# Attention on one core: two key tiles per stretch of values, a score bank copied out by VectorE, keys split later

## The chip, the cores and the metric

The kernel runs on one core of a Trainium2 chip. The metric is the device time of one execution in microseconds (us). TensorE (PE, its weight loads PEld), VectorE (DVE), ScalarE (ACT), GpSimd (POOL) and SyncE (SP, which issues most DMAs) each take their own instructions in order and wait for one another by semaphores. Matmul results land in PSUM, eight banks of 128x512 fp32.

## The reference

```python
def _A_ref(x, wq, wk, wv, wo):            # x 1x2048x448, 16 heads of 28, one shared key and value head
    q = (x @ wq).reshape(B, S, H, Dh).transpose(0, 2, 1, 3)
    k = x @ wk
    v = x @ wv
    scores = jnp.einsum("bhqd,bkd->bhqk", q, k) * (Dh ** -0.5)
    p = softmax(scores)
    o = jnp.einsum("bhqk,bkd->bhqd", p, v)
    return o.transpose(0, 2, 1, 3).reshape(B, S, H * Dh) @ wo

def _B_ref(x, w1, w2, w3, w4):
    h = gelu(layernorm(x) @ w1)
    hs = token_shift(h) @ w2              # four channel groups, moved by +1, -1, +2, -2 tokens
    x1 = x + hs
    return x1 + gelu(layernorm(x1) @ w3) @ w4

g = sigmoid((x * gate_w).sum(-1, keepdims=True))
return g * _A_ref(x, ...) + (1 - g) * _B_ref(x, ...)
```

All is fp32.

## The kernel before

The order of every engine's instructions is the order in which the code writes them; nothing is rearranged. Most matmuls are made of three faster ones (fp32r): an operand is split into a high part `h` and a low part `l`, and high x high, high x low and low x high are added up.

**Start, 0 to about 130 us.** Queries, keys, values and the mixer's first half. Queries with keys and values in their spare rows go to DRAM (`qd`). `stage_w2` for the third token block calls `third(t)` between its tiles. There `load_k(b)` (eight DMAs, L332) reads a quarter of the keys from `qd` into one buffer `kf`, and `split_k(b)` on GpSimd (L336, L337) writes `kH` and `kL` from it. `stage_w2` for the last block calls `weights(t)`: it splits the first chunks of the MLP's weights (`split_w3`, in which GpSimd clears a part of `w3h`, L106) and issues the loads of the next (`load_w34`, L550).

**MLP, about 130 to 420 us.** Four blocks `b` of 512 tokens; in each, 14 tiles `f`: `w3_part` (11 matmuls, L130 to L134, two gelus), and for tile `f - 2` `w4_part` (12 matmuls). In tiles 10 and 11, DVE normalises the next block through the buffer `xn`. In block 1, `khd` (a few keys of each head) is put together, the first query tile is loaded and split; from block 2 on, `fill` does the parts of the first unit's maximum.

**Attention, from about 420 us.** 16 units `u`, each four heads by 512 queries, 16 key tiles `kt` of 128 keys. For each key tile there are 12 score matmuls (three splits, four heads side by side in row tiles of the array), into four of seven banks in rotation (`bank` takes the first of the list and puts it at its end). ScalarE takes the exponential of each bank (L832) into a tile `p`. `pv_group` multiplies `p` of the key tile two before with the values, in fp32, four heads side by side in column tiles, adding up over all 16 key tiles in an eighth bank. Beside that, in key tiles set by lists:

- `max_part` (four a unit) and `max_end` make a bound on the next unit's scores from 64 keys, which goes into spare rows of `qh` by DMA.
- After a unit, `sums_begin` copies the result to `o` and sends the sums by DMA; `recip` in key tile 3 and `norm` in key tile 6 divide by them. The reciprocals make a round trip through DRAM (`rd`, `rb`). GpSimd then splits the result.
- `wo_job` (three fp32r matmuls, four times a unit) is the output projection; DVE adds it up in `ot` (L778). In unit 0 four leftovers of the MLP, `w4_job`, stand in its place.

The end divides the last unit by another way, tests whether any sum was too large, and holds a branch that computes attention again with a full maximum.

Of the kernel before, what the change touches and what calls it, by code (L numbers as in the profile page):

```python
# [9 lines left out]
F32 = mybir.dt.float32  # L10
# [6 lines left out]
P = 128  # L17
# [15 lines left out]
MK = 64  # L33
# [3 lines left out]
def f32(ap):  # L37
    return ap.bitcast(F32)
# [3 lines left out]
def gated_mix_kernel(  # L42
# [41 lines left out]
    def mm_tile(name):  # L84
        return psA.tile([P, 512], F32, tag="mm", bufs=2, name=name)
# [114 lines left out]
    def max_part(u, t, tile_of):  # L200
        if t == 0:
            mx_of[u] = late.tile([P, 4, 4], F32, tag="mr", bufs=1, name=f"mr_{u}")
        ps = tile_of(f"m_{u}_{t}")[:, 0:4 * MK].rearrange("p (j k) -> p j k", j=4)
        nc.tensor.matmul(ps, qh_of[u][:, t * P:(t + 1) * P], khd, start=True, stop=True)  # L204
        nc.vector.reduce_max(mx_of[u][:, :, t], ps, axis=AX.X)  # L205
# [32 lines left out]
    with tc.tile_pool(name="s1b", bufs=1) as s1b, \  # L238
# [77 lines left out]
        kf = s1b.tile([P, 512], F32, name="kf")  # L316
        nc.gpsimd.memset(kf, 1.0)

# [9 lines left out]
        def load_k(b):  # L328
            for r in range(4):
                for g, n in ((0, 16), (1, DH - 16)):  # L330
                    at = 32 * r + 16 * g
                    nc.sync.dma_start(kf[at:at + n, :], rest(g, n, b))  # L332

        def split_k(b):
            cols = slice(512 * b, 512 * b + 512)
            nc.gpsimd.tensor_copy(kH[:, cols], kf)  # L336
            nc.gpsimd.tensor_tensor(kL[:, cols], kf, f32(kH)[:, cols], ALU.subtract)  # L337
# [191 lines left out]
        load_k(0)  # L529
# [77 lines left out]
    with tc.tile_pool(name="s2", bufs=1, reuse_waits="tile") as s2, \  # L607
# [5 lines left out]
        fills = [lambda t=t: max_part(0, t, max_tile if t % 2 else misc_tile) for t in range(4)]  # L613
        fills += [lambda: max_end(0)]
# [30 lines left out]
        for b in range(NB):  # L645
            acc = [ps2.tile([P, 512], F32, tag="acc", bufs=4, name=f"acc_{b}_{t}") for t in range(4)]
            gs = {}
            for f in range(NF):
# [24 lines left out]
                if b == 1 and f == 1:  # L673
# [4 lines left out]
                if b == 1 and f == 5:  # L678
                    q_split(0, qh0, ql0)
                if f >= 2:  # L680
                    for t in range(4):
                        w4_part(f - 2, t, gs[f - 2], acc)
                        if b > 1 and t % 2 == 0 and f < NF - 1:
                            fill()
# [15 lines left out]
    with tc.tile_pool(name="s3", bufs=1, reuse_waits="tile") as s3, \  # L700
            tc.tile_pool(name="ps3", bufs=1, space=PSUM, reuse_waits="tile") as ps3:
        woh = s3.tile([P, 4, D], F32R, name="woh")
        wol = s3.tile([P, 4, D], F32R, name="wol")

        banks = [mm_tile("bank_0"), mm_tile("bank_1"), misc_tile("bank_2")]
        banks += [ps3.tile([P, 512], F32, name=f"bank_{i}") for i in range(3, 7)]

# [26 lines left out]
        def sums_begin(u, pv):  # L734
            o = s3.tile([P, 512], F32, tag="o", bufs=2, name=f"o_{u}")
            nc.vector.tensor_copy(o, pv)
# [15 lines left out]
        def norm(u, o, rb):  # L752
            on = s3.tile([P, 512], F32, tag="onf", bufs=2, name=f"on_{u}")
            nc.vector.tensor_mul(on, o, rb)  # L754
            onh = s3.tile([P, 512], F32R, tag="onh", bufs=2, name=f"onh_{u}")
            onl = s3.tile([P, 512], F32R, tag="onl", bufs=2, name=f"onl_{u}")
            nc.gpsimd.tensor_copy(onh, on)  # L757
            nc.gpsimd.tensor_tensor(onl, on, f32(onh), ALU.subtract)
            on_of[u] = (onh, onl)
# [3 lines left out]
        def wo_job(u, t, end=None):  # L763
            b, g = divmod(u, NG)
            n = 4 * b + t
            tok = slice(t * P, (t + 1) * P)
            onh, onl = on_of[u]
            ps = bank(f"job_{n}")[:, 0:D]
            nc.tensor.matmul(ps, onh[:, tok], woh[:, g, :], start=True, stop=False)  # L769
            nc.tensor.matmul(ps, onh[:, tok], wol[:, g, :], start=False, stop=False)  # L770
            nc.tensor.matmul(ps, onl[:, tok], woh[:, g, :], start=False, stop=True)  # L771
# [3 lines left out]
            if end:  # L775
                end(t, n, ps, before)
                return
            nc.vector.scalar_tensor_tensor(ot_of[n], ps, gg[:, n:n + 1], before, op0=ALU.mult, op1=ALU.add)  # L778
            if g == NG - 1:
                nc.sync.dma_start(out[0, n * P:(n + 1) * P, :], ot_of[n])  # L780

        woraw = s3.tile([P, 4, D], F32, name="woraw")
        nc.sync.dma_start(woraw, wo.rearrange("(g p) n -> p g n", p=P))
        nc.gpsimd.tensor_copy(woh, woraw)
        nc.gpsimd.tensor_tensor(wol, woraw, f32(woh), ALU.subtract)
# [13 lines left out]
        p_of, pv_of, sums, norms = {}, {}, [], []  # L799

        def pv_group(k):
            u, kt = divmod(k, NT)
            if kt == 0:
                pv_of[u] = max_tile(f"pv_{u}")
            pv = pv_of[u]
            ps = p_of.pop(k)
            for j in range(4):
                nc.tensor.matmul(pv[32 * j:32 * j + 32, :], vext[:, kt, :], ps[j],  # L808
                                 start=(kt == 0), stop=(kt == NT - 1), tile_position=(0, 32 * j))
            if kt == NT - 1 and u < NU - 1:  # L810
                sums.append(sums_begin(u, pv_of.pop(u)))

        WO_AT = (8, 10, 12, 14)
        M_AT = (1, 3, 4, 5)
        M_FIRST = (5, 7, 9, 10)
        LAG = 2

        for k in range(NU * NT + LAG):
            u, kt = divmod(k, NT)
            if k < NU * NT:  # L820
                if kt == 13 and u + 2 < NU:
                    q_begin(u + 2)
                    q_fetch(u + 3)
                bs = [bank(f"s_{4 * k + j}") for j in range(4)]
                for i in range(3):
                    for j in range(4):
                        for _, _, w, a in score(u, bs[j], j, slice(kt * P, (kt + 1) * P), i=i):
                            nc.tensor.matmul(bs[j], w, a, start=(i == 0), stop=(i == 2), tile_position=(32 * j, 0))  # L828
                p_of[k] = []
                for j in range(4):  # L830
                    p = s3.tile([P, 512], F32, tag="p", bufs=PB, name=f"p_{4 * k + j}")
                    nc.scalar.activation(p, bs[j], AF.Exp, scale=SCALE)  # L832
                    p_of[k].append(p)
                if kt == 3 and sums:
                    norms.append(recip(*sums.pop()))
                if kt == 6 and norms:
                    norm(*norms.pop())
                if kt in WO_AT:
                    t = WO_AT.index(kt)
                    if u:  # L840
                        wo_job(u - 1, t)
                    else:
                        w4_job(t)
                m_at = M_AT if u else M_FIRST
                if u + 1 < NU and kt in m_at:
                    t = m_at.index(kt)
                    max_part(u + 1, t, bank)
                    if t == 3:
                        max_end(u + 1)
            if k >= LAG:  # L850
                pv_group(k - LAG)
# [3 lines left out]
        pv = pv_of.pop(u)  # L855
        o = s3.tile([P, 512], F32, tag="o", bufs=2, name=f"o_{u}")
        onh = s3.tile([P, 512], F32R, tag="onh", bufs=2, name=f"onh_{u}")
        onl = s3.tile([P, 512], F32R, tag="onl", bufs=2, name=f"onl_{u}")
        on_of[u] = (onh, onl)
# [18 lines left out]
        def tail_back(t):  # L878
            nc.tensor.transpose(tq[t], on4[:, t], ident)
            nc.scalar.copy(onh[:, toks[t]], tq[t])  # L880

        def tail_low(t):
            nc.vector.tensor_sub(onl[:, toks[t]], tq[t], f32(onh)[:, toks[t]])
# [20 lines left out]
        for t in range(4):  # L904
            nc.scalar.copy(o[:, toks[t]], pv[:, toks[t]])
# [14 lines left out]
        tail_low(0)  # L920
        tail_on(3)
        tail_low(1)
# [6 lines left out]
        tail_low(2)  # L929
        tail_wo(0)  # L930
        tail_back(3)
        tail_low(3)
        tail_wo(1)
        tw = max_tile("worst_t")[0:1, 0:P]
# [10 lines left out]
        with tc.If(again > 0, label="redo"):  # L945
            for b in range(NB):
                for g in range(NG):
# [5 lines left out]
                    pv = max_tile(f"pv2_{u}")  # L953
# [9 lines left out]
                    norm(*recip(*sums_begin(u, pv), False))  # L963
                    for t in range(4):
                        wo_job(u, t)
# [51 lines left out]
```

## Time and profile before

| | |
|---|---|
| median of 3 runs | 994.31 us (994.22 to 994.57) |
| profiled execution | 995.8 us |
| its span, first to last instruction | 994.0 us |
| mean granted TensorE clock over the span | 0.989 |
| TensorE, ScalarE, VectorE, GpSimd busy | 970.8, 651.9, 287.1, 107.5 us |

Names in the lines shown: a row of the timeline gives start, duration, engine, line, operation, tiles written <- tiles read, shapes and count; in brackets the idle time before it and what ended it. A window's row gives its length, the busy time of PE, PEld, DVE, ACT and POOL with instruction counts, the granted clock, the DMA share and GB/s. A group's row gives busy time, mean ns of one, and the idle time of its engine before it. Each fp32 matmul shows as two records, its passes. A busy TensorE is not one at its peak, as matmuls overlap.

### The profile page before, as it was taken

To read this page: it belongs to the slowest core of one execution; us is meant where nothing else is said; L and a number is where in the kernel's file an instruction comes from. 1 tells how busy PE (TensorE), PEld (TensorE's weight loads), DVE (VectorE), ACT (ScalarE), POOL (GpSimd) and SP (SyncE) were. 2 spreads that over 40 slices of the span, in tenths; PEclk is the share of its full clock that TensorE was granted. 3 is DMA by queue.
4 is the path that set the end of the run, shared out by engine and by line. 5 is a ranking of instruction groups with operands and counts; after the bars stand their busy time and mean duration, and the time that the engine had idled before them with its cause. 6 is when DMAs were issued, how large, how long until landed. Compare 5 with 4: busy or idle time off the path is not lost.

```text
span 994.0 us, 18445 instructions
## 1 busy us (share of the span) xinstructions
PE 970.8 (98%) x7251; PEld 562.5 (57%) x7251; DVE 287.1 (29%) x572; ACT 651.9 (66%) x1266; POOL 107.5 (11%) x134
## 2 busy tenths in 40 slices
PE   9999949999999999999999999999999999999997
PEld 6788838888888888843333333333333333333333
DVE  4663424631431431212222222212222221222112
ACT  5542315432232232299999999999998999999895
POOL 2241320100000520040000000000000000000000
PEclk9999969999999999999999999999999999999999
DMA  9703334130210300010000010000010000110001
GB/s 322 244 27 79 114 98 121 44 87 1 40 41 2 77 3 11 1 49 24 13 24 14 19 54 13 24 13 20 27 41 23 14 24 12 42 33 3 12 13 41
DMA packets 38750, 46.19 MB, mean 46 GB/s; under 512 B 8880, under 2 KB 27008, under 8 KB 38656
## 3 DMA queue, kind: packets, MB, share of 16 engines
q1 hardware_dynamic: 35632, 39.47, 13.4%
q10 hardware_dynamic: 3024, 5.47, 1.6%
q8 instruction: 59, 0.97, 0.4%
q14 instruction: 35, 0.29, 0.1%
HBM read 32.85 MB, written 11.67 MB: 45 GB/s over the span
## 4 chain that ended last, share of the span: by engine, by line
PE 94%; DMA 2%; SPq 1%; POOL 1%; DVE 0%; issue 0%; ACT 0%; POOLq 0%; DVEq 0%; ACTq 0%
PE pv L808 25%; PE bank L828 23%; PE acc L642 4%; PE acc L641 4%; PE acc L643 4%; PE g L131 4%; PE g L132 4%; PE g L130 4%; PE bank L769 2%; PE bank L204 2%; SPq L332 1%; PE g L133 1%; PE bank L771 1%; PE g L134 1%; PE bank L770 1%; PE h L130 1%
## 5 line engine op out<-in xcount | busy, mean ns | idle before, releaser
L832 ACT ACTIVATE p<-bank 128x512 f32<-128x512 f32 x1024 | 515.3, 640 | 47.9 <-PE bank L828 45.6
L808 PE MATMUL pv<-p,vext 128*32 128x512 f32 x2048 | 272.9, 604 | 0.0
L828 PEld LDWEIGHTS bank<-qh,kH 30*128 30x128 f32 x1024 | 51.7, 181 | 214.4 <-ACT p L832 212.9
L631 ACT ACTIVATE gh<-g 128x512 fp32r<-128x512 f32 x55 | 32.8, 597 | 183.6 <-PE g L134 183.6
L828 PE MATMUL bank<-qh,kH 30*128 30x512 f32 x1024 | 133.1, 494 | 0.4 <-ACT p L832 0.4
L828 PE MATMUL bank<-qh,kL 28*128 28x512 f32 x1024 | 105.7, 391 | 0.0
L828 PE MATMUL bank<-ql,kH 28*128 28x512 f32 x1024 | 105.6, 388 | 0.0
L633 DVE TENSOR_TENSOR gl<-gf,gh 128x512 fp32r<-128x512 f32 x55 | 38.5, 700 | 165.3 <-ACT gf L632 165.3
L808 PEld LDWEIGHTS pv<-p,vext 128*32 128x32 f32 x2048 | 40.6, 108 | 76.5 <-issue 62.8
L642 PE MATMUL acc<-w4l,gh 128*128 128x448 f32 x220 | 80.4, 366 | 0.0
L641 PE MATMUL acc<-w4h,gh 128*128 128x448 f32 x220 | 80.3, 365 | 0.0
L643 PE MATMUL acc<-w4h,gl 128*128 128x448 f32 x220 | 80.2, 365 | 0.0
L778 DVE SCALAR_TENSOR_TENSOR ot<-bank,gg,ot 128x448 f32<-128x448 f32 x44 | 30.1, 684 | 161.2 <-PE bank L771 122.6
L131 PE MATMUL g<-al,w3h 128*128 128x512 f32 x168 | 66.4, 395 | 0.0
L205 DVE TENSOR_REDUCE mr<-bank 128x4 f32<-128x256 f32 x60 | 25.6, 426 | 141.2 <-PE bank L204 141.2
L130 PE MATMUL g<-ah,w3h 128*128 128x512 f32 x168 | 66.3, 395 | 0.0
L132 PE MATMUL g<-ah,w3l 128*128 128x512 f32 x168 | 66.3, 395 | 0.0
L757 POOL CAST onh<-on 128x512 fp32r<-128x512 f32 x15 | 9.2, 611 | 493.0 <-DVE on L754 458.7
L828 PEld LDWEIGHTS bank<-ql,kH 28*128 28x128 f32 x1024 | 52.6, 185 | 9.1
L828 PEld LDWEIGHTS bank<-qh,kL 28*128 28x128 f32 x1024 | 51.9, 185 | 0.0
L641 PEld LDWEIGHTS acc<-w4h,gh 128*128 128x128 f32 x220 | 41.3, 188 | 4.7
L642 PEld LDWEIGHTS acc<-w4l,gh 128*128 128x128 f32 x220 | 41.3, 188 | 4.1
(196 smaller groups left out, 1096.2 us busy)
## 6 DMA issues: line engine op xcount, KB each, us to landing
qd<-qf ACTq DMA_DIRECT2D x16, 256.0 KB
qr<-qd SPq DMA_DIRECT2D x16, 256.0 KB
rb<-rd SPq DMA_DIRECT2D x15, 256.0 KB
x<-in_x_dram SPq DMA_DIRECT2D x4, 896.0 KB
xd<-xt SPq DMA_DIRECT2D x16, 224.0 KB
w34raw<-in_w_dram SPq DMA_DIRECT2D x7, 512.0 KB
out_dram<-ot SPq DMA_DIRECT2D x15, 224.0 KB
w34raw<-in_w_dram SPq DMA_DIRECT2D x7, 448.0 KB
```

The costliest lines, as they stand in the source:

```text
L130: nc.tensor.matmul(ps, wh[:, c, :], ah[:, c, :], start=(c == 0), stop=False)
L131: nc.tensor.matmul(ps, wh[:, c, :], al[:, c, :], start=False, stop=False)
L132: nc.tensor.matmul(ps, wl[:, c, :], ah[:, c, :], start=False, stop=False)
L631: nc.scalar.activation(gh, ps, AF.Gelu_apprx_tanh)
L633: nc.vector.tensor_sub(gl, gf, f32(gh))
L641: nc.tensor.matmul(ps, gh[:, tok], w4h[i][:, k, :], start=(f == 0), stop=False)
L642: nc.tensor.matmul(ps, gh[:, tok], w4l[i][:, k, :], start=False, stop=False)
L643: nc.tensor.matmul(ps, gl[:, tok], w4h[i][:, k, :], start=False, stop=(f == stop))
L778: nc.vector.scalar_tensor_tensor(ot_of[n], ps, gg[:, n:n + 1], before, op0=ALU.mult, op1=ALU.add)
L808: nc.tensor.matmul(pv[32 * j:32 * j + 32, :], vext[:, kt, :], ps[j], start=(kt == 0), stop=(kt == NT - 1), tile_position=(0, 32 * j))
L828: nc.tensor.matmul(bs[j], w, a, start=(i == 0), stop=(i == 2), tile_position=(32 * j, 0))
L832: nc.scalar.activation(p, bs[j], AF.Exp, scale=SCALE)
```

## The change

- A *stretch* `v` is now two key tiles: 24 score matmuls, then what else is due, then the 8 value matmuls (16 records) of the stretch before. Their result, over two key tiles, is copied or added to `o` in SBUF by DVE (L826, L828) at once.
- All eight banks are in one list. `take` removes the first; it is put back at the end when the code writes its last reader.
- Of the four score banks of a key tile, one (head 3) is copied to its `p` by DVE (L808), and ScalarE takes that exponential in place in SBUF, after the other six of the stretch (`late_exps`, L815).
- The output projection is one fp32 matmul in four column tiles of 32 tokens in place of three fp32r ones; the splits of `wo` and of the result go away. The load of `wo` moves ahead of the query loads.
- The maximum takes 32 keys in place of 64, all four parts in one bank with one reduction, in stretch 2 of the unit before. `recip` is in stretch 2, `norm` in stretch 3, `wo_job` in stretches 4 to 7.
- Keys are loaded and split in MLP block 1 (tiles 0 to 7), through `xn`; `khd` and the first query tile in block 2; the first maximum in block 3.

```diff
-MK = 64
+MK = 32
-    def max_part(u, t, tile_of):
...
+    def max_all(u, ps):
+        mx_of[u] = late.tile([P, 4, 4], F32, tag="mr", bufs=1, name=f"mr_{u}")
+        for t in range(4):
+            nc.tensor.matmul(ps[:, t * P:(t + 1) * P], qh_of[u][:, t * P:(t + 1) * P], khd, start=True, stop=True)
+        nc.vector.reduce_max(mx_of[u].rearrange("p j t -> p t j"), ps.rearrange("p (t j k) -> p t j k", t=4, j=4), axis=AX.X)
...
-        def load_k(b):
+        def load_k(b, kf):
+            kf_of[b] = kf
+            nc.gpsimd.memset(kf, 1.0)
...
-            split_k(t) if t < 2 else None
-            load_k(t + 1) if t < 2 else None
...
-        split_k(2)
-        load_k(3)
-        split_k(3)
...
+                if b == 1 and f in (0, 2, 4, 6):
+                    load_k(f // 2, s2a.tile([P, 512], F32, tag="xn", bufs=1, name=f"kf_{f // 2}"))
+                if b == 1 and f in (1, 3, 5, 7):
+                    split_k(f // 2)
...
+        wof = s3.tile([P, 4, D], F32, name="wof")
+        nc.sync.dma_start(wof, wo.rearrange("(g p) n -> p g n", p=P))
-        banks = [mm_tile("bank_0"), mm_tile("bank_1"), misc_tile("bank_2")]
+        banks = [mm_tile("bank_0"), mm_tile("bank_1"), misc_tile("bank_2"), max_tile("bank_7")]
...
         def wo_job(u, t, end=None):
...
+            ps = take()
+            for j in range(4):
+                tok = slice(t * P + 32 * j, t * P + 32 * j + 32)
+                nc.tensor.matmul(ps[32 * j:32 * j + 32, 0:D], on_of[u][:, tok], wof[:, g, :],
+                                 start=True, stop=True, tile_position=(0, 32 * j))
...
+        def exps(u, kt, bs):
+            ps = p_of[u, kt] = {}
+            for j in READ:
+                ps[j] = s3.tile([P, 512], F32, tag="p", bufs=PB, name=f"p_{u}_{kt}_{j}")
+                if j in DRAIN:
+                    nc.vector.tensor_copy(ps[j], bs[j])
+                else:
+                    nc.scalar.activation(ps[j], bs[j], AF.Exp, scale=SCALE)
+                banks.append(bs[j])
+        def late_exps(u, kt):
+            for j in DRAIN:
+                nc.scalar.activation(p_of[u, kt][j], p_of[u, kt][j], AF.Exp, scale=SCALE)
+        def values(u, v, add=True):
+            pv = take()
+            for kt in (2 * v, 2 * v + 1):
...
+        READ = (0, 3, 1, 2)
+        DRAIN = (3,)
+        WO_AT = (4, 5, 6, 7)
+        M_AT = 2
+        for k in range(NU * NV):
+            u, v = divmod(k, NV)
+            if v == 6 and u + 2 < NU:
+                q_begin(u + 2)
+                q_fetch(u + 3)
+            for kt in (2 * v, 2 * v + 1):
+                exps(u, kt, scores(u, kt))
+            for kt in (2 * v, 2 * v + 1):
+                late_exps(u, kt)
+            if v == 2 and sums:
+                norms.append(recip(*sums.pop()))
+            if v == 3 and norms:
+                norm(*norms.pop())
+            if v == M_AT and u + 1 < NU:
+                ps = take()
+                max_all(u + 1, ps)
+                banks.append(ps)
+                max_end(u + 1)
+            job = None
+            if v in WO_AT:
+                if u:
+                    job = wo_job(u - 1, WO_AT.index(v))
+                else:
+                    w4_job(WO_AT.index(v))
+            if job:
+                wo_add(*job)
+            if k:
+                values(*divmod(k - 1, NV))
+                if v == 0:
+                    sums.append(sums_begin(u - 1, o_of[u - 1]))
```

More of the change, by code (lines that the diff above doesn't have):

```diff
@@ L752, in norm @@
         def norm(u, o, rb):
[L753 to L759, printed above, removed]
+            on_of[u] = s3.tile([P, 512], F32, tag="on", bufs=2, name=f"on_{u}")
+            nc.vector.tensor_mul(on_of[u], o, rb)
         ot_of = {}
@@ L775, in wo_job, with wo_add @@
             if end:
-                end(t, n, ps, before)
+                end(t, n, ps[:, 0:D], before)
+                banks.append(ps)
                 return
-            nc.vector.scalar_tensor_tensor(ot_of[n], ps, gg[:, n:n + 1], before, op0=ALU.mult, op1=ALU.add)
+            return n, g, ps, before
+        def wo_add(n, g, ps, before):
+            nc.vector.scalar_tensor_tensor(ot_of[n], ps[:, 0:D], gg[:, n:n + 1], before, op0=ALU.mult, op1=ALU.add)
+            banks.append(ps)
             if g == NG - 1:
                 nc.sync.dma_start(out[0, n * P:(n + 1) * P, :], ot_of[n])
[L782 to L785, printed above, removed]
         weigh_x1(NT - 4, NT)
@@ L797, in w4_job @@
             nc.vector.scalar_tensor_tensor(x1[:, n, :], ps, gi[:, n:n + 1], x1[:, n, :], op0=ALU.mult, op1=ALU.add)
[L799 to L829, printed above, removed]
-                for j in range(4):
[L831 to L851, printed above, removed]
@@ new lines, in gated_mix_kernel, with scores @@
+        p_of, o_of, sums, norms = {}, {}, [], []
+        NV = 8
+        def scores(u, kt):
+            bs = [take() for j in range(4)]
+            for i in range(3):
+                for j in range(4):
+                    for _, _, w, a in score(u, bs[j], j, slice(kt * P, (kt + 1) * P), i=i):
+                        nc.tensor.matmul(bs[j], w, a, start=(i == 0), stop=(i == 2), tile_position=(32 * j, 0))
+            return bs
+        def exps(u, kt, bs):
[7 more added lines that the diff above has]
+                banks.append(bs[j])
@@ new lines, in late_exps @@
+        def late_exps(u, kt):
[4 more added lines that the diff above has]
+            for kt in (2 * v, 2 * v + 1):
+                ps = p_of.pop((u, kt))
+                for j in range(4):
+                    nc.tensor.matmul(pv[32 * j:32 * j + 32, :], vext[:, kt, :], ps[j],
+                                     start=(kt % 2 == 0), stop=(kt % 2 == 1), tile_position=(0, 32 * j))
+            if v == 0:
+                o_of[u] = s3.tile([P, 512], F32, tag="o", bufs=2, name=f"o_{u}")
+                nc.vector.tensor_copy(o_of[u], pv)
+            elif add:
+                nc.vector.tensor_add(o_of[u], o_of[u], pv)
+            else:
+                return pv
+            banks.append(pv)
```

65 lines of the change are left out of this document (24 added, 41 removed).

## The prediction

> **What bounds the kernel now.** I read the page first, then the attention stage (420 to 982 us) by windows and timeline, then the stage boundary where the clock drops.
>
> ```profile
> span 994.0 us, 18445 instructions
> PE 970.8 (98%) x7251; PEld 562.5 (57%) x7251; DVE 287.1 (29%) x572; ACT 651.9 (66%) x1266; POOL 107.5 (11%) x134
> L832 ACT ACTIVATE p<-bank 128x512 f32<-128x512 f32 x1024 | 515.3, 640 | 47.9 <-PE bank L828 45.6
> 600.00:700.00 100.00, 100.00 (x963) 38.16 (x959) 22.14 (x49) 91.82 (x183) 5.68 (x6) 1.00 0.06 18
> 750.01 1.00 PE pv L808 x8
> 784.97 1.00 PE pv L808 x8
> ```
>
> The last two rows are the same place of two successive units (a unit is one head group by 512 queries): 34.96 us. TensorE has no idle in the window, but ScalarE is 92% busy: it is a second limit close behind. The timeline shows what a key tile costs TensorE:
>
> ```profile
> 600.65 0.51 PE L828 MATMUL bank<-qh,kH 30*128 30x512 f32 x4
> 600.99 0.41 PE L828 MATMUL bank<-qh,kL 28*128 28x512 f32 x4
> 601.22 0.40 PE L828 MATMUL bank<-ql,kH 28*128 28x512 f32 x4
> 601.55 0.39 PE L204 MATMUL bank<-khd,qh 128*128 128x256 f32 x1
> 601.87 1.06 PE L808 MATMUL pv<-p,vext 128*32 128x512 f32 x8
> 602.86 0.51 PE L828 MATMUL bank<-qh,kH 30*128 30x512 f32 x4
> 978.31 1.92 PE L808 MATMUL pv<-p,vext 128*32 128x512 f32 x16
> ```
>
> Starts count, since matmuls overlap. Scores: .34 to the second group, .23 to the third, .32 to the next kind; values .99 (two passes of four tiles); a max part .32. A plain tile is .89+.99, about 1.9. Of this some .1 is paid at each change of kind. The last row is from the end, where tiles' values follow each other: 8 records take 1.06, 16 take 1.92, so 8 more add .86 and a pass is .43; the last one before scores is .99-.45, some .54. Values of two tiles in a row are then 3x.43+.54, 1.84, against 1.98.
>
> **Boundary before the MLP.** The keys are loaded through one buffer, and GpSimd's split waits for each load, ahead of the clearing of `w3h` that TensorE needs.
>
> ```profile
> 114.30 25.75 SPq L332 DMA_DIRECT2D kf<-qd  x24
> 133.03 1.27 POOL kL L337
> 142.57 1.27 POOL kL L337
> 143.89 0.32 POOL w3h L106
> 144.25 0.79 PE g L133
> PE g L133 <- POOL w3h L106: 13.6, 1, 13.6
> 128.00:130.40 2.40, 2.40 (x12) 1.86 (x10) 0.00 (x0) 0.00 (x0) 0.00 (x0) 1.00 0.12 37
> 132.40:133.40 1.00, 0.00 (x0) 0.00 (x0) 0.00 (x0) 0.00 (x0) 0.92 (x2) 0.76 0.00 0
> 144.20:149.90 5.70, 5.65 (x13) 4.46 (x14) 3.56 (x7) 3.46 (x6) 1.25 (x5) 0.50 0.65 222
> 140.16 0.61 SPq L550 DMA_DIRECT2D w34raw<-in_w_dram  x1
> 144.70 0.83 ACT L105 CAST w3h<-w34raw 128x768 fp32r<-128x768 f32 x1 [24.11 <-DMA w34raw<-in_w_dram]
> ```
>
> TensorE's wait is 13.6 after the modelled end of the matmul before, 13.8 counted from starts: it stops at 130.4. The window 132.4 to 133.4 has a mean granted clock of .76, so it halved near 132.9, 2.5 us after the stop; the 13 matmuls of the next 5.7 us take .43 in place of .23 (11 of them in 2.5 us before), 2.7 more. With the splits moved, nothing on GpSimd stands ahead of the clearing. Next late is the second weight load, which stood behind the key loads on SP's queue (114.30 to 140.05): from its issue at 140.16 to its use at 144.70 it took 4.5. It otherwise waits only for the split of the first block, which the projection running at 128 has behind it. So it is there by 132.9 at the latest, and TensorE wants it after two more `f`, 2x2.5 after 128.4, at 133.4, with its splits of some 2 us in between. I take the whole, as the issue is likelier well before 128: **-16.5**, and -14 as the other end.
>
> The moved steps are 32 small DMAs, four memsets and eight GpSimd operations in MLP block 1.
>
> ```profile
> 204.03 1.34 SPq L173 DMA_DIRECT2D xr<-xd  x2
> 258.16 0.51 DVE L158 TENSOR_SCALAR xn<-x,mv_s2a,rs_s2a 128x448 f32<-128x448 f32 x1
> ```
>
> They share SP's queue with nothing from 205.4 until the next write of `xt`, GpSimd's with `rs` and `khd`. Their buffer `xn` is wanted again at 258.2. Four rounds at some 10 us (133.03 to 142.57, and a memset) end about 246: covered, 0; if not, DVE's normalising waits and block 2 starts late. `khd`, the first query load and split go from block 1 to 2 and the first unit's max from block 2 to 3, still ahead of their first use after 418: 0, the four max parts there being at most 1.3 us with their .32 each. GpSimd's splits of `wo` and of each `on` go away; they were off the path, as TensorE never idled for them: 0.
>
> **Stretch by stretch in attention.** TensorE runs 24 scores, an extra, then the values of the stretch before. As built, the extra, or else the values, takes the bank that the stretch's first exponential has just read: a loop through both engines.
>
> ```profile
> 628.19 0.40 PE L828 MATMUL bank<-ql,kH 28*128 28x512 f32 x4
> 628.68 0.60 ACT L832 ACTIVATE p<-bank 128x512 f32<-128x512 f32 x1 [0.58 <-PE bank L828]
> 420.77 12.38 ACT L832 ACTIVATE p<-bank 128x512 f32<-128x512 f32 x25 [3.37 <-PE bank L828]
> 115.97 2.19 ACT L574 CAST ah<-xr 128x512 fp32r<-128x512 f32 x4 [5.41 <-DMA xr<-xd]
> 110.67 0.60 PE L342 MATMUL vp<-ident,vT 128*128 128x128 f32 x4
> ```
>
> ScalarE: a run of 25 exponentials from PSUM takes 12.38, so .49 each. From SBUF no exponential is in the trace; the nearest row is four casts in 2.19, .525 each ((2.19-.62)/3); bounds .477 (the closest starts from PSUM) and .63 (no overlap). Six at .49 and two at .525 make **4.0** a stretch. The copy to SBUF thus saves ScalarE nothing; it frees a bank early. TensorE's own sum is .79+.78+1.84 = 3.4, so plain stretches are ScalarE's.
>
> The Trainium skill ("ScalarE: Activation LUTs", What ACT_TABLE_LOAD costs) gives 186 ns + .833 a column less 93 of overlap, .52, with no word on the source; by it a stretch would be 4.16, three plain ones .5 a unit more, and the result 8 us later. The run of 25 says .49 from PSUM, and the measurement decides.
>
> With an output job, the loop is: first exponential .60 and release .05; job; values 1.84; scores to exponential .34+.23+.49 = 1.06. The job is now two passes of 448 columns, .76 by the values' rate, where three fp32r ones stood (about .8 each, four a unit both ways, so no saving). 4.31, four times a unit. A max stretch is 3.55 plus four 128-column matmuls; the nearest row, four transposes, steps .11, hence .54 and 4.09; bounds 4.0 (hidden) and 4.83 (four at .32). Before, max cost four such parts, 1.28 a unit.
>
> DVE gets two copies, one add and other work a stretch:
>
> ```profile
> 633.09 0.61 PE L808 MATMUL pv<-p,vext 128*32 128x512 f32 x4
> 633.77 0.69 DVE L736 COPY o<-pv 128x512 f32<-128x512 f32 x1 [0.60 <-PE pv L808]
> 601.49 0.24 DVE L745 RECIPROCAL rr<-rt 128x16 f32<-128x16 f32 x1
> 608.30 0.69 DVE L754 TENSOR_TENSOR on<-o,rb 128x512 f32<-128x512 f32 x1 [0.64 <-DMA rb<-rd]
> L754 DVE TENSOR_TENSOR on<-o,rb 128x512 f32<-128x512 f32 x15 | 10.4, 693 | 19.0 <-DMA rb<-rd 19.0
> ```
>
> Four operations of .69, 2.8 of 4 us, fit. **A new wait** does not. From the reciprocal's end to the landing of `rb` is 6.57 us; before, DVE waited 1.3 a unit for it (19.0/15) and nothing stood behind. Now `norm` comes one stretch after `recip`, and behind it stand the add that frees the values' bank and the copies of scores. Counting from the first exponential of stretch 2: (a plain stretch's add ends .65+1.84-.54+.66+.69 = 3.3 after its first exponential; the next second scores start at 3.4, which is -.6 here; third group .45, .49 to DVE, copy .69) its second copy ends at 1.0, the reciprocal at 1.4, `rb` lands at 8.0, which is 3.9 into stretch 3 (4.09 long before it). `norm` and add, .70+.69, free the bank at 5.3 instead of 3.4. The second scores of stretch 4 start there; scores .78, job .76, values 1.84, 1.06: stretch 5 begins at 9.75 instead of 4.0+4.31. **+1.4** a unit (1.0 to 2.2 over `rb` of 6.2 to 7.4). Later stretches can't catch up, their loop is longer than ScalarE's work.
>
> Unit: 3x4.0+4.09+4x4.31+1.4 = 34.7 against 34.96. Sixteen units, the first without norm (-1.4), the last without max in both: before 558.1, after 554: **-4**.
>
> **Start of attention.** The load of `wo` now stands ahead of that of the second query tile, and as built waits for the MLP's last matmul. The split of that tile is on DVE ahead of the first copies, which free banks.
>
> ```profile
> 419.48 0.36 PE L643 MATMUL acc<-w4h,gl 128*128 128x448 f32 x1
> 421.59 0.34 SPq L178 DMA_DIRECT2D qr<-qd  x1
> 427.00:428.00 1.00, 1.00 (x16) 0.60 (x12) 0.00 (x0) 1.00 (x4) 0.00 (x0) 1.00 0.24 91
> 420.87 0.69 DVE L184 TENSOR_TENSOR ql<-qr,qh 128x512 fp32r<-128x512 f32 x1
> ```
>
> The same two transfers took from 421.59 until just before 428 (DMA share .24 in the last microsecond). Issued at 419.9, when the quoted matmul ends, they are there by 426.1; the split is two operations of at most .69, say 1.2; copy .69, release and scores 1.1: stretch 1 begins at 429.1 instead of 420.77+4.0, 4.3 late. TensorE, done with stretch 0's scores at 421.3, is idle over 6 us, so the clock halves as at 132.9, and half of the next 5.7 us is lost, 2.85, less the .6 a stretch by which TensorE is ahead: 2.1. **+6.4** (3 if `qr` overtakes `wo`, 9 if not).
>
> The tail changes by an exponential and an add more, less the low halves: +.3 (-1 to +1).
>
> **Sum.** -16.5-4+6.4+.3 = -13.8 on a span of 994.0: 980.2. The profiled execution took 995.8, 1.8 around its span; the median of the runs is 994.31, 1.5 less. Taken from the median: **980.5**.
>
> **Rivals.**
> - *The clock halves at each norm wait* (slower). TensorE's gap there is about 1.9 us (3.4 to 5.3); at 130.4 the clock halved 2.5 after the stop. An `rb` over .6 later crosses it. Then half of 5.7 us (row 144.20:149.90) is lost in job stretches, which have no slack: 2.85x15 = 43, 1023 us. It decides from `rb` at 7.2 us on. For: the waits differ by unit. Against: the .6 of margin, and 6.57 in the unit quoted. Chance .10.
> - *Short idles alone halve the clock* (slower). TensorE now pauses .6 in each plain stretch. If that put four of a unit's eight stretches at half clock, each would take 2x3.4 instead of 4.2, 10 a unit, 160 in all, 1140 us. Against: the only halving quoted needed 2.5 us of stop. Chance .02. The Trainium skill ("TensorE: Matmul & The Clock Gate", A second HAM failure mode: psum-queue depth-cycling) says that short idles between groups that cycle through PSUM banks do this; no row of this trace shows it, since TensorE has no idle there.
> - *Engines decouple* (faster): banks let TensorE run ahead, and the norm wait hides. ScalarE's 8x4.0 = 32 is then the unit: 2.7x16, some 42 less, 938. For: ScalarE's total exceeds TensorE's (27.2 and 3.5 of extras). Against: the bank order above. Chance .07.
> - *Late keys collide*: with rounds of 13 us or more instead of 10 the cover to 258.2 is gone; `xn` late by 5 to 8: 987. Chance .07.
> - *Long stretches*, at the upper bound of each term (max 4.83, jobs 4.4 to 4.6, norm 2.2): unit 35.5 to 36.3, +13 to +26: 994 to 1006. Chance .13.
>
> **How the numbers follow.** Forecast .61, by itself 968 to 993 (unit 33.9 to 35.4, start 3 to 9, boundary -14 to -16.5). The range also takes in most of the long stretches: 962 to 1001; left out are the two clock rivals, the decoupled engines and the last of the long stretches, .2. A measurement of this kernel can tell .2%, 2 us. Slower: .12 of the clock and .07 of the long stretches, .19; same: .05 from between; faster: .76.
>
> **What would show it.** Right: no gap of TensorE before 150, so the stage begins 16 us earlier; after its first eight exponentials a hole of some 4 us with DVE waiting for `qr`, at half clock; a unit period near 34.7; DVE waiting over 2 us a unit for `rb`, with TensorE's largest gap right behind it; ScalarE near 92% busy; eight exponentials in 4.0. Wrong: half clock inside units; a period near 32 or over 35.5; TensorE waiting in block 2 for `ah`; exponentials from SBUF starting .6 apart.

## The result and the profile after

Over 20 runs each, the changed kernel takes 999.96 us in the median (994.52 to 1005.12) and the kernel before 995.20 (993.72 to 996.64): a ratio of 1.0048, 95% interval 1.0035 to 1.0061, slower by half a per cent. The forecast was 980.5 and faster. The direction was wrong; the range of 962 to 1001 holds the result, but by luck, since its upper part stood there for long stretches and the clock rivals were left out of it. The profiled execution took 1000.73 with a span of 998.9, 4.9 more than the span of 994.0 before. The runs of the changed kernel also lie ten us apart where those of the kernel before lie three apart; that turns out to belong to the answer. In the quickest of them (994.52 and 995.28) the mean granted clock is .986, in the longest (1005.12) .980.

The profile's page, totals and costliest group of the kernel after (busy us, mean ns of one, idle before it and its releaser):

```profile
PE 955.4 (96%) x7571; PEld 580.8 (58%) x7571; DVE 515.9 (52%) x892; ACT 653.5 (65%) x1262; POOL 74.8 (7%) x105
L810 ACT ACTIVATE p<-bank 128x512 f32<-128x512 f32 x768 | 394.4, 638 | 62.2 <-PE bank L800 60.9
```

Within attention TensorE now has idle time (from 412 to 983.7 it is busy for 541.95 of 571.70 us), and most of it is in one place: 24.1 us on the add of L828. The waits of the kernel after name both halves of it (us in total, times, longest):

```profile
DVE on L753 <- DMA rb<-rd: 38.1, 15, 3.2
PE bank L800 <- DVE o L828: 24.1, 15, 2.3
```

DVE waits fifteen times for `rb`, once per unit but the first, and fifteen times TensorE then waits 1.6 us on average for the bank that the add behind `norm` frees. The timeline of one unit of the kernel after shows the step, with two more rows of `norm`:

```profile
532.41 0.69 DVE L753 TENSOR_TENSOR on<-o,rb 128x512 f32<-128x512 f32 x1 [2.61 <-DMA rb<-rd]
533.02 0.68 DVE L828 TENSOR_TENSOR o<-o,bank 128x512 f32<-128x512 f32 x1
533.76 0.49 PE L800 MATMUL bank<-qh,kH 30*128 30x512 f32 x1 [1.70 <-DVE o L828]
...
569.22 0.69 DVE L753 TENSOR_TENSOR on<-o,rb 128x512 f32<-128x512 f32 x1 [2.49 <-DMA rb<-rd]
...
604.07 0.69 DVE L753 TENSOR_TENSOR on<-o,rb 128x512 f32<-128x512 f32 x1 [2.19 <-DMA rb<-rd]
```

From 569.22 to 604.07 the period is 34.85, close to the forecast of 34.7. From 532.41 to 569.22 it is 36.81. What makes the difference is in the windows of the kernel after (length, then busy time and count of PE, PEld, DVE, ACT, POOL, then the mean granted clock):

```profile
120.00:150.00 30.00, 30.00 (x141) 26.16 (x140) 15.91 (x30) 12.55 (x22) 0.55 (x2) 1.00 0.51 163
494.31:497.72 3.41, 1.09 (x15) 0.65 (x17) 1.99 (x4) 2.04 (x5) 0.00 (x0) 1.00 0.06 14
497.72:501.14 3.42, 3.42 (x20) 0.87 (x16) 1.28 (x2) 2.35 (x5) 0.00 (x0) 0.50 0.00 0
531.86:535.27 3.41, 1.71 (x20) 0.78 (x21) 2.42 (x4) 2.64 (x6) 0.00 (x0) 1.00 0.01 1
535.27:538.68 3.41, 3.41 (x20) 0.64 (x12) 0.84 (x2) 1.92 (x4) 0.00 (x0) 0.50 0.00 0
603.54:606.95 3.41, 2.13 (x28) 0.93 (x24) 2.43 (x4) 3.04 (x7) 0.00 (x0) 1.00 0.04 8
606.95:610.37 3.42, 3.42 (x44) 1.60 (x36) 1.89 (x4) 2.31 (x5) 0.00 (x0) 1.00 0.00 0
818.57:821.99 3.42, 2.28 (x32) 1.24 (x32) 1.89 (x3) 3.21 (x8) 0.00 (x0) 1.00 0.06 13
```

The first row is the old stop before the MLP: it is gone, as forecast. The rows behind it are pairs. In the first of a pair lies the stop behind `norm`; where TensorE is busy for 1.09 or 1.71 of 3.41 us, the whole next window is granted half clock (20 matmuls instead of 44); where it is busy for 2.13, it is not. Near that value the rows don't agree: 2.28 at 818.57 was followed by half clock. Eight units have such a window, all of about 3.41 us. They lie on one grid: from 497.72 to 535.27 are 37.55 us, 11 times 3.413. The periods that hold a half window average 36.91, the other six 35.05 (their sum is 965.03 - 459.43, first to last `norm`), so a halving costs 1.86 by this trace, and eight cost 15. That is most of the 18.7 us by which the span missed its forecast of 980.2. Counted from the first instruction, the grid lies elsewhere in another execution: in the kernel with the split later, below, a half window starts at 407.40, which is 90.32 or 26.46 windows ahead of 497.72. So which units are hit can change from run to run, and this fits the wide spread.

The Trainium skill ("TensorE: Matmul & The Clock Gate", What's actually happening) says that the clock is decided over free-running windows of 3413 ns, and this trace agrees, to 3.413. Its section Why this matters for your kernels speaks of stops over some 3 us, and here the measurement differs: stops of 1.14 to 2.32 were enough in eight units, while those of 1.03 to 1.57 in the other seven were not.

### The profile page after: what moved, and what is told of

Read it like the earlier page. It is cut to its first block, busy times and chain, and to the rows that moved or that the text cites. A ratio compares the mean times of both kernels' runs of the same rounds, so it can differ in the third digit from the quotient of the medians.

```text
span 998.9 us, 19201 instructions
## 1 busy us (share of the span) xinstructions
PE 955.4 (96%) x7571; PEld 580.8 (58%) x7571; DVE 515.9 (52%) x892; ACT 653.5 (65%) x1262; POOL 74.8 (7%) x105
## 3 DMA queue, kind: packets, MB, share of 16 engines
q1 hardware_dynamic: 35632, 39.45, 13.3%
## 5 line engine op out<-in xcount | busy, mean ns | idle before, releaser
L810 ACT ACTIVATE p<-bank 128x512 f32<-128x512 f32 x768 | 394.4, 638 | 62.2 <-PE bank L800 60.9
L822 PE MATMUL bank<-p,vext 128*32 128x512 f32 x2048 | 255.7, 618 | 2.5 <-ACT p L810 1.1
L808 DVE COPY p<-bank 128x512 f32<-128x512 f32 x256 | 175.3, 690 | 43.9 <-PE bank L800 35.6
L800 PE MATMUL bank<-qh,kH 30*128 30x512 f32 x1024 | 146.9, 458 | 29.6 <-DVE o L828 24.1
L800 PEld LDWEIGHTS bank<-qh,kH 30*128 30x128 f32 x1024 | 73.2, 183 | 164.5 <-ACT p L810 53.1
L815 ACT ACTIVATE p<-p 128x512 f32<-128x512 f32 x256 | 154.9, 692 | 3.5 <-DVE p L808 3.5
L822 PEld LDWEIGHTS bank<-p,vext 128*32 128x32 f32 x2048 | 60.8, 113 | 141.3 <-issue 109.1
L800 PE MATMUL bank<-qh,kL 28*128 28x512 f32 x1024 | 131.2, 399 | 0.0
L800 PE MATMUL bank<-ql,kH 28*128 28x512 f32 x1024 | 128.9, 391 | 0.0
L828 DVE TENSOR_TENSOR o<-o,bank 128x512 f32<-128x512 f32 x111 | 76.2, 686 | 94.3 <-PE bank L822 93.0
L763 PE MATMUL bank<-wof,on 128*32 128x448 f32 x512 | 65.3, 585 | 0.3
```

The source lines that it names most:

```text
L808: nc.vector.tensor_copy(ps[j], bs[j])
L810: nc.scalar.activation(ps[j], bs[j], AF.Exp, scale=SCALE)
L815: nc.scalar.activation(p_of[u, kt][j], p_of[u, kt][j], AF.Exp, scale=SCALE)
L828: nc.vector.tensor_add(o_of[u], o_of[u], pv)
```

## The experiments

Each is an edit of the changed kernel, except that of the keys alone. The kernel before, timed beside them again, took 995.48 or 994.87 in the median where it had taken 995.20, so a difference from 999.96 is uncertain by some tenths of a us for this alone. Theory A was that the wait behind `norm` costs twice, its own length and the half-clock windows that follow it.

**Norm behind the add.**

```diff
-            if v == 3 and norms:
-                norm(*norms.pop())
...
                 if v == 0:
                     sums.append(sums_begin(u - 1, o_of[u - 1]))
+            if v == 3 and norms:
+                norm(*norms.pop())
```

> The changed kernel with one move: `norm` is recorded behind the stretch's add instead of ahead of it, so that no bank waits for `rb`. Theory A (the stop of TensorE behind `norm` costs twice, by itself and by a window at half clock): the stop of 1.6 us a unit and the eight windows of 3.41 us at half clock go, the unit falls from 36.1 on average to 33.3 to 33.5, time 957 to 963. Rival B (the stretches themselves are longer than forecast, and half clock comes of TensorE's short pauses anywhere): halvings go on, unit over 35, time 994 or more. Rival C (only the clock was lost, the wait was made up for by later stretches): unit 34.8, time 978 to 983.

Measured: 968.02 (966.21 to 968.77), ratio to before .9717 (.9703 to .9732), so 32 us less than as built. First and last `norm` and a wait of this kernel:

```profile
459.54 0.69 DVE L753 TENSOR_TENSOR on<-o,rb 128x512 f32<-128x512 f32 x1 [0.33 <-DMA rb<-rd]
...
932.81 0.69 DVE L753 TENSOR_TENSOR on<-o,rb 128x512 f32<-128x512 f32 x1 [0.57 <-DMA rb<-rd]
```

```profile
PE bank L763 <- DVE on L753: 3.3, 4, 1.5
```

No unit has a half clock. The period is (932.81 - 459.54)/14 = 33.8; theory A gave 33.3 to 33.5, and missed by 5 us, 3.3 of them since `rb` is late for the output job in four units. Rivals B and C fall: they gave 994 or more, and 978 to 983. The runs lie 2.6 us apart.

**The stop filled, the wait kept.**

```diff
+        NFILL = 12
...
             for kt in (2 * v, 2 * v + 1):
+                if kt == 9 and u:
+                    for _ in range(NFILL):
+                        nc.tensor.matmul(banks[0][:, 0:256], warm[:, 0:P], warm, start=True, stop=True)
                 exps(u, kt, scores(u, kt))
```

> The changed kernel with twelve matmuls on constants of 256 columns each (about 1.3 us) put on TensorE in each unit but the first, between the two groups of scores behind `norm`: the wait for `rb` and the late bank stay, only TensorE's idle is filled. Their result is overwritten. Theory A (half clock comes of the idle there, and the wait costs its own 1.4 a unit beside it): no half clock in any unit, all fifteen periods 34.6 to 35.2, time 979 to 984. Rival B (half clock comes of the shorter pauses anywhere in the stretches): halvings go on as before, 997 to 1003. Rival D (the halvings are a symptom and cost nothing, the long units have another cause): halvings gone, periods of 36 to 37 stay, 997 to 1003.

Measured: 987.65 (986.54 to 991.00), .9924 (.9909 to .9940). The timeline of this kernel at one `norm`, then its first and last, and what is left of the stop:

```profile
566.05 1.48 PE L847 MATMUL bank<-warm 128*128 128x256 bf16 x12
566.32 0.69 DVE L753 TENSOR_TENSOR on<-o,rb 128x512 f32<-128x512 f32 x1 [2.23 <-DMA rb<-rd]
567.47 0.69 PE L800 MATMUL bank<-qh,kH 30*128 30x512 f32 x4
...
460.88 0.69 DVE L753 TENSOR_TENSOR on<-o,rb 128x512 f32<-128x512 f32 x1 [2.88 <-DMA rb<-rd]
...
953.67 0.69 DVE L753 TENSOR_TENSOR on<-o,rb 128x512 f32<-128x512 f32 x1 [2.82 <-DMA rb<-rd]
```

```profile
PE bank L800 <- DVE o L828: 3.8, 4, 1.9
```

DVE still waits. TensorE has no hole at this `norm`; a part of the stop is left in four units (3.8 us in all, in place of 24.1 in fifteen). In the profiled execution no unit is at half clock, and the period is 492.79/14 = 35.2. This is theory A, some 4 us over its range of 979 to 984: three periods are 35.9 to 37.1, the other eleven 34.7 to 35.2. So the clock is worth 12.3 us (999.96 to 987.65), and the wait itself 19.6 (to 968.02), or 1.3 a unit. The 12.3 make 1.5 for each of eight halvings, a little less than the 1.86 of the one trace above. The run of 991.00 had a mean clock of .990 in place of .994 to .995, so units may still have been hit in it. Rival B, by which the halvings go on, and rival D, by which they cost nothing, fall.

**A longer stop.**

```diff
+            rd2 = dram.tile([4, 512], F32, tag="rd2", bufs=2, name=f"rd2_{u}")
+            nc.sync.dma_start(rd2, rd)
...
-            nc.sync.dma_start(rb, rd.unsqueeze(1).broadcast_to([4, 32, 512]))
+            nc.sync.dma_start(rb, rd2.unsqueeze(1).broadcast_to([4, 32, 512]))
```

> The changed kernel with one transfer more between `rd` and `rb` in every unit but the first (DRAM to DRAM, 8 KB, some 1.5 to 2.5 us by the 1.4 us between the issues of `rd` and `rb`), so that the stop behind `norm` grows from 1.0 to 2.3 us to some 3 to 4.5. Theory A (the granted clock halves for one 3.41-us window after a window in which TensorE stood idle for about 1.6 us or more; whether a unit is hit depends on where the stop lies against the windows): such a stop has 1.6 us in one window wherever it lies, so all fifteen units have a half clock, some of them two windows; period 38.5 to 40, time 1035 to 1060. Rival F (the units that halve are those with another fault, and a longer stop costs its own length only): 8 of 15 still, period 36.1 + 2, time 1025 to 1032. Rival G (the wait is made up for by later stretches): 1000 to 1010.

Measured: 1050.82 (1049.18 to 1051.07), 1.0556 (1.0540 to 1.0572). Three neighbouring windows of this kernel, and its wait:

```profile
497.12:500.54 3.42, 0.50 (x11) 0.07 (x3) 0.00 (x0) 2.28 (x5) 0.00 (x0) 1.00 0.24 80
500.54:503.95 3.41, 1.66 (x13) 0.92 (x17) 1.89 (x3) 0.34 (x1) 0.00 (x0) 0.50 0.01 2
503.95:507.36 3.41, 3.41 (x20) 0.91 (x24) 1.38 (x2) 2.27 (x5) 0.00 (x0) 0.50 0.00 0
```

```profile
PE bank L802 <- DVE o L830: 53.1, 15, 5.0
```

The stop is 3.5 on average (53.1/15). All fifteen units have a half clock, eight of them two windows of it, as theory A had it; rivals F (1025 to 1032) and G (1000 to 1010) fall. The spread is small too, 2 us over four runs.

**The split of the second query tile later.**

```diff
-        q_begin(1)
-        q_fetch(2)
...
+            if k == 1:
+                q_begin(1)
+                q_fetch(2)
```

> The changed kernel with one move: the split of the second query tile (and the load of the third) stands behind stretch 1 instead of ahead of stretch 0, so that the first copies of scores don't wait for `qr`; the load of `wo` stays where it is. Theory (the start stall is as forecast): the hole of 5.5 us in TensorE at 405 goes, no half clock at 409, the second stretch's first exponential comes 4.0 after the first's instead of 7.9, time 5 to 6.5 us less, 993.5 to 995. Rival (the wait comes back two stretches later, where the max of the second unit needs the split, or the four stretches make it up anyway): less than 2 us, 998 to 1000.

Measured: 992.70 (988.72 to 996.61), .9969 (.9954 to .9983), 7.3 less than as built. The timelines of the kernel after and then of this one, at the start of attention:

```profile
403.93 3.04 ACT L810 ACTIVATE p<-bank 128x512 f32<-128x512 f32 x6 [3.37 <-PE bank L800]
408.72 0.43 DVE L183 CAST qh<-qr 128x512 fp32r<-128x512 f32 x1 [5.07 <-DMA qr<-qd]
410.53 0.80 PE L800 MATMUL bank<-qh,kH 30*128 30x512 f32 x3 [5.46 <-DVE p L808]
411.81 1.58 ACT L810 ACTIVATE p<-bank 128x512 f32<-128x512 f32 x3
...
443.44 1.09 ACT L810 ACTIVATE p<-bank 128x512 f32<-128x512 f32 x2 [0.38 <-PE bank L800]
```

```profile
403.30 3.04 ACT L808 ACTIVATE p<-bank 128x512 f32<-128x512 f32 x6 [3.37 <-PE bank L798]
...
407.22 1.12 ACT L808 ACTIVATE p<-bank 128x512 f32<-128x512 f32 x2
...
438.34 1.08 ACT L808 ACTIVATE p<-bank 128x512 f32<-128x512 f32 x2 [0.35 <-PE bank L798]
```

```profile
407.40:410.81 3.41, 2.90 (x16) 0.59 (x16) 0.69 (x1) 3.41 (x8) 0.00 (x0) 0.50 0.02 5
```

The second stretch begins 3.92 after the first in place of 7.88: the stall is gone. The expectation of no half clock there failed, as the last row, a window of this kernel, shows. The first unit takes 438.34 - 403.30 = 35.0 in place of 39.5, so 4.5 of the gain lie there. The rest of the 7.3, a little over the 5 to 6.5 expected, is not shown; both kernels are hit by halvings in their units (eight in each trace) and spread by 8 to 10 us.

**Keys alone, on the kernel before.** `load_k` and `split_k` go to block 1, `khd` and the first query tile to block 2, the first maximum to block 3, as in the change; attention stays as before.

```diff
-            split_k(t) if t < 2 else None
-            load_k(t + 1) if t < 2 else None
...
-        split_k(2)
-        load_k(3)
-        split_k(3)
...
+                if b == 1 and f in (0, 2, 4, 6):
+                    load_k(f // 2, s2a.tile([P, 512], F32, tag="xn", bufs=1, name=f"kf_{f // 2}"))
+                if b == 1 and f in (1, 3, 5, 7):
+                    split_k(f // 2)
```

> The kernel before with one part of the change alone: keys loaded and split in MLP block 1, the first query tile and its max one block later; attention as before, with its four max parts of 64 keys and all exponentials from PSUM. Theory (the boundary is worth 16.5 and the moved work costs nothing): no stop of TensorE at 130 to 144 and no half clock there, attention begins 16 to 17 us earlier, time 978 to 979.5. Rival (part of it is given back, by late keys in blocks 1 and 2 or at the start of attention): 981 to 990.

Measured: 979.85 (978.58 to 981.35), .9842 (.9828 to .9856): 15.6 less than before. A window of this kernel:

```profile
120.00:150.00 30.00, 30.00 (x141) 26.18 (x140) 16.14 (x30) 12.55 (x22) 0.56 (x2) 1.00 0.50 162
```

The stop and its half clock are gone. It came out between the theory (978 to 979.5) and the rival (from 981). The trace has one window at half clock at the start of attention, and the last section shows the window ahead of it. The two of the five runs whose mean clock, .999, leaves no room for one took 978.58 and 979.55, close to the theory.

**Three moves together**: `norm` behind the add, the reciprocal behind the add of stretch 1, the split later.

```diff
-            if v == 2 and sums:
-                norms.append(recip(*sums.pop()))
...
+            if v == 1 and sums:
+                norms.append(recip(*sums.pop()))
+            if v == 3 and norms:
+                norm(*norms.pop())
+            if k == 1:
+                q_begin(1)
+                q_fetch(2)
```

> The changed kernel with three moves: `norm` behind the add, the reciprocal one stretch earlier (behind the add of stretch 1), the split of the second query tile behind stretch 1. Theory: the move of `norm` gave 968.0 and its unit still has 4.68 instead of 4.39 in stretch 4 on average, for three late `rb`; the earlier reciprocal takes 4 us off the wait, so the unit is 33.5, and -0.3x15 = -4.5; the split gives another 5 to 7: 955 to 959, stretches 3.92, 3.92, 4.25, 3.92 and four of 4.4, no half clock between the start and the tail. Rival (the reciprocal now waits for `rt` and holds up the copies behind it, or the split is in the way of stretch 2): 960 to 968.

Measured: 957.43 (956.31 to 957.76), .9620 (.9607 to .9633): faster than both kernels, by 3.8% and 4.3%. Window, first and last `norm` of this kernel:

```profile
444.00:911.00 467.00, 460.32 (x4975) 202.11 (x4968) 305.20 (x515) 449.48 (x893) 0.00 (x0) 1.00 0.08 23
```

```profile
453.39 0.68 DVE L751 TENSOR_TENSOR on<-o,rb 128x512 f32<-128x512 f32 x1
...
922.25 0.69 DVE L751 TENSOR_TENSOR on<-o,rb 128x512 f32<-128x512 f32 x1
```

The period is 468.86/14 = 33.49, with no wait for `rb` in either row, and the clock is full. TensorE is busy for 98.6% and ScalarE for 96.2% of the window: both are nearly full.

**No copies.** `DRAIN = ()` in place of `DRAIN = (3,)`, with the three moves.

> The three moves, and all eight exponentials of a stretch read PSUM; DVE copies nothing. Theory A (as the forecast has it, the copy saves ScalarE no time; what it frees early is not needed, since a plain stretch is eight exponentials and a job stretch a loop that begins with the first one): plain stretches 3.9, job stretches 4.4, time as with the three moves, within 4 us of 957. Rival B (the banks freed by the copies are what lets the second scores start in time): every stretch longer by up to one exponential, .49, so 0.2 to 0.5 x 128 = 25 to 63 us more, 980 to 1020.

Measured: 970.74 (970.24 to 971.38), .9755 (.9742 to .9769), 13.3 more than with the copies. The same wait with the three moves, and then without copies:

```profile
PEld bank L798 <- ACT p L808: 66.7, 82, 0.8
```

```profile
PEld bank L798 <- ACT p L808: 129.1, 210, 1.7
```

Scores now wait for ScalarE 210 times in place of 82. Neither expectation is right: the copies are worth .83 a unit (13.3/16), more than nothing and much less than an exponential a stretch. By the medians over the units, a plain stretch is even shorter without them (3.83 against 3.92); the loss is largest in stretch 4 (4.81 against 4.35) and in the max stretch (4.51 against 4.25). That a bank freed early is what makes it good fits the waits; why it is so uneven stays open.

**The extra behind the values**: output job and max recorded behind `values` and what follows it, with the three moves.

> The three moves, and the extra of a stretch (output job or max) stands behind the values instead of ahead of them. Theory H (a job stretch is the loop of first exponential, job, values, scores, 4.38, and with the job out of the loop it is TensorE's own sum, 24 scores 1.57, job .76, values 1.84 = 4.17): 0.2 less in 64 stretches, 12 to 13 us less than with the three moves, 943 to 947. Rival I (the job now stands between the values and the next scores and takes the same place in the loop, by another bank): no gain, or up to 0.2 more a stretch, 955 to 970.

Measured: 956.95 (956.27 to 957.41), .9617 (.9604 to .9630), the same as with the three moves. The timeline of one job stretch of this kernel:

```profile
567.57 3.05 ACT L808 ACTIVATE p<-bank 128x512 f32<-128x512 f32 x6 [0.30 <-PE bank L798]
568.27 1.92 PE L820 MATMUL bank<-p,vext 128*32 128x512 f32 x16
570.01 0.94 PE L761 MATMUL bank<-wof,on 128*32 128x448 f32 x8
571.94 1.09 ACT L808 ACTIVATE p<-bank 128x512 f32<-128x512 f32 x2 [0.30 <-PE bank L798]
```

Now the values take the bank that the first exponential has read (.70 after its start), the job follows, and it is 4.37 from exponential to exponential. Both stand between it and the next scores whichever comes first; rival I held, theory H fell.

## Why the prediction was wrong, step by step

- *Boundary, -16.5: right.* The first exponential starts at 403.93, where the kernel before had it at 420.77, so -16.84. Keys alone gave -15.6 in the median.
- *Moved keys, 0: right.* TensorE is busy for all 253.90 us from 150 to 403.90, so nothing was late by them; the rival of late keys did not come.
- *Stretches: right within .2.* With the three moves the medians are 3.92 for plain ones (4.0 forecast), 4.25 with the max (4.09), 4.35 to 4.40 with a job (4.31). The unit without the wait came to 33.5 where 34.7 - 1.4 = 33.3 was forecast. Exponentials from SBUF were taken at the right price: six from PSUM took 3.05 (567.57, in the kernel with the extra behind the values), where one takes .64, so .48 from start to start, and 3.92 - 6x.48 leaves .52 for each of the two from SBUF.
- *The wait behind norm, +1.4 a unit: right.* The experiments give it 1.3. Units without a half window take 35.05 in place of 34.7.
- *Start, +6.4: right.* The second stretch is 3.9 late, at 411.81, and the first unit takes 443.44 - 403.93 = 39.5, where 33.3 + 6.4 = 39.7 was forecast.
- *Tail, +.3: mis-sized.* It is 1.7. Rows of before, then of after:

```profile
978.47 2.07 ACT L832 ACTIVATE p<-bank 128x512 f32<-128x512 f32 x4 [0.58 <-PE bank L828]
984.08 0.45 PE L769 MATMUL bank<-woh,onh 128*128 128x448 f32 x1
986.62 0.37 PE L771 MATMUL bank<-woh,onl 128*128 128x448 f32 x1
```

```profile
982.53 1.19 ACT L815 ACTIVATE p<-p 128x512 f32<-128x512 f32 x2
987.89 0.96 PE L763 MATMUL bank<-wof,on 128*32 128x448 f32 x8
990.12 1.71 PE L763 MATMUL bank<-wof,on 128*32 128x448 f32 x16
```

  From the last exponential's end (980.54, and 983.72) the first output job comes 3.54 later before and 4.17 after, the last one ends 6.45 and 8.11 later. So .6 lies ahead of the first job, where the values are longer and an add is new, and 1.0 in the four jobs themselves; what makes either was not tried.
- *The clock behind norm: this step failed.* The rival stood there, with its mechanism and its place, at a chance of .10, "from `rb` at 7.2 us on", since the clock before had halved 2.5 us after a stop. The 2.5 was the place of one stop on a grid, taken for a length that a stop must have. Windows of the kernel before, laid on its own grid, show it:

```profile
129.51:132.92 3.41, 1.11 (x5) 0.56 (x4) 0.00 (x0) 0.00 (x0) 0.58 (x1) 1.00 0.08 24
132.92:136.33 3.41, 0.00 (x0) 0.00 (x0) 0.00 (x0) 0.00 (x0) 1.29 (x2) 0.50 0.03 10
```

  There too the clock halved behind a window in which TensorE was busy for 1.11 us. In the units what sorts the stops, outside a band of values that the last section gives, is how much of a 3.41-us window stays idle: the average stop of 1.6, which is less than the 1.9 that the prediction worked out, is enough where nearly all of it falls into one window. The margin of .6 was none, and an `rb` of 7.2 us was not needed: in five of the eight units that were hit, `norm` started within 6.9 us of the reciprocal's end. The rival's price was too high in turn: by the trace 1.86 in eight units, 15 in all, not 43, since the half clock lasted one window there, not 5.7 us, and seven units were not hit.

Spans: -16.8 at the boundary, then 579.8 against 559.8 from first to last exponential (+20.0), +1.7 in the tail, sum +4.9. Forecast for the middle was +2.4; with eight halvings of 1.86 it would have been +17.3.

The rival of short idles alone did not come: the window with the three moves has 6.7 us of idle in 467, by modelled ends, and a clock of 1.00. The rule of the Trainium skill that the prediction named beside it ("TensorE: Matmul & The Clock Gate", A second HAM failure mode: psum-queue depth-cycling) is not borne out by this window. Nor is the .52 that its page "ScalarE: Activation LUTs" gives, for exponentials from PSUM: they took .48, and plain stretches 3.92, not 4.16; for those from SBUF it fits. The engines did not decouple.

## What to carry to other kernels

An operation that waits for a transfer belongs behind everything on its engine that frees a buffer, not ahead of it: one move was worth 32 us here. A stop of the matmul engine is to be priced by its share of a clock window, not by whether it is longer than the last stop seen to halve the clock, and where it can be split by the grid, the price is a chance per stop. A run-to-run spread that grows with a change is a hint of this before the trace is read.

## What the runs showed of the hardware that was not expected

In the kernel after and those with the longer stop and the split later, the clock halved behind every full-clock window of the units in which TensorE was busy for 1.83 us or less of 3.41, and never behind one where it was busy for more than 2.28. Between, both occur: 2.28 at 818.57 was followed by half clock, 2.13 at 603.54 was not, nor was 1.93 at 741.91 in the kernel with the split later. What decides between them is open.

In the units the half clock lasted one window, or two where TensorE was idle for a part of the first, even for .2 us. The first row, from the kernel with the longer stop, is such a window; the second, from the same kernel, is a case to the contrary behind the units:

```profile
1012.54:1015.95 3.41, 3.20 (x21) 1.36 (x25) 1.45 (x3) 1.88 (x4) 0.00 (x0) 0.50 0.02 5
1039.84:1043.26 3.42, 1.53 (x16) 0.26 (x8) 1.72 (x4) 0.39 (x1) 1.16 (x1) 1.00 0.46 169
```

The first was followed by another window at half clock. At the start of attention it was otherwise: TensorE was idle for .5 of the half-clock window at 407.40 that is shown above, and the next was full. In the second row, among the last output jobs, TensorE was busy for 1.53 only, and the next window was granted in full. So the busy time of the profile, whose ends of matmuls are modelled, sorts the windows of the units and not all others.

At the start of attention the clock also halved behind windows that the profile shows as busy, in the kernels with keys alone, with the split later, without copies and with the extra behind the values. The one with keys alone:

```profile
404.28:407.69 3.41, 3.04 (x28) 1.51 (x25) 0.68 (x1) 3.41 (x8) 0.00 (x0) 1.00 0.40 66
```

The 28 records are few: 24 scores elsewhere take 1.57, so 28 are about 1.8 us of work by estimate, which would put this window on the same side. But with the three moves a window there (406.27 to 409.69) holds 29 and the clock stayed full, so the estimate doesn't settle it, and it was not tried by itself.
